# A pooled-and-banded attention kernel feeding a phase mixer: the pooled branch is added to the transposed banded one, the mixer works in 128-token chunks, and inputs are staged in pieces

## The chip, the cores and the metric

The kernel runs on one NeuronCore of a Trainium2 chip. TensorE (PE, with its weight loads shown apart as PEld) does the matrix products and writes to PSUM; VectorE (DVE) and ScalarE (ACT) read PSUM and SBUF; GpSimd (POOL) works in SBUF; SyncE (SP) issues the transfers. Each engine takes its instructions in the order in which they stand. The metric is the device time of one execution in microseconds.

## The reference

There are 8 batches of 8 heads, 576 tokens and 64 features per head. Two attentions are added, and the sum goes through a mixer over tokens and a product over channels:

```python
q_d, k_d, v_d = (t.reshape(B, H, 144, 4, 64).mean(axis=3) for t in (q, k, v))
out_up    = repeat(softmax(q_d @ k_d.T / 8) @ v_d, 4, axis=2)      # pooled by 4 tokens
out_local = softmax(where(|i - j| < 4, q @ k.T / 8, -1e9)) @ v     # banded
x = (out_up + out_local) as (B, 576, 512)
theta = x @ w_theta
zr, zi = x * cos(theta), x * sin(theta)
y = w_tok_r @ zr + w_tok_i @ zi                                    # over tokens
u = x + y
out = u + maximum(u @ w_ch, 0)
```

Inputs and output are float32; the kernel's products take bf16 and sum in float32.

## The kernel before, in words

Each batch passes through ten step functions, all of them generators whose every `yield` is one step. `load` issues the transfers of q, k and v, `cast` makes bf16 of them (GpSimd, in batch 0 also VectorE), `turns` transposes q and k by matmuls against a matrix `ip` that holds an identity and 24 pooling columns, so that each chunk of 96 tokens gives 96 transposed tokens and 24 pooled ones (lines 331 to 335). Batches 0 and 1 are read in another layout and are pooled by six more matmuls of 144 columns per pair of heads (line 312). `turns` ends with the pooled values, five matmuls of 512 columns (line 349).

`scores` makes the pooled scores in two groups of 90 and 54 keys (line 368), exponentiates them on ScalarE (lines 379, 388), then does the same for the band in five overlapping windows of 128 keys (lines 400, 408) and sets everything outside the band to zero by two selections on GpSimd (lines 421, 423), in batch 0 and part of batch 1 by one multiplication on VectorE. `pooled_out` multiplies the pooled weights with the pooled values (line 437, 32 matmuls per batch). `outputs` works in five chunks of 120, 120, 120, 120 and 96 tokens: one matmul of 512 columns spreads the pooled result over its tokens (line 462, `psup`), eight small ones give the banded result (line 467), and VectorE divides (476) and adds the two (483) to get `x`, tokens on partitions.

`transposes` turns `x` into `xT` (500, 505), `phases` multiplies by `w_theta` (517) and takes the cosine and the sine on ScalarE (524, 525), `modulate` multiplies both by `x` on VectorE (533). `mix` does the product over tokens: eight groups per batch, each of ten matmuls of 288 columns, five chunks times two matrices (553), and VectorE adds `xT` (559). `channels` multiplies by `w_ch` and transposes back (573, 578; the last 64 tokens as two halves side by side, 586 and 593), ScalarE clips at zero (598), and `store` adds and writes out (608, 610). `build_WT` loads, casts and transposes the two token matrices once (254 to 283).

What sets the order is written out by hand: strings of letters, `FIRST` and `SECOND` for the first two batches, `PERIOD` for each of the middle ones, `LAST` and `END`. Each letter takes one step of one function: `l`, `k`, `L` load, `C` cast, `A` turns, `S` scores, `N` pooled_out, `V` outputs, `T` transposes, `H` phases, `Z` modulate, `X` mix, `R` channels, `O` store, `W` the token matrices. `pin` ties every instruction to the one before it on its engine, so the letters fix the order on each engine. In a round for batch b the letters `X`, `R` and `O` stand for batch b-1, `A` for b+1, `C` for b+2 and `L` for b+3. PSUM has two tiles of two banks (`w2`) and four of one bank (`w1`), each handed out in turn.

## Time and profile before

| What | Value |
|---|---|
| Time, median of 3 runs | 298.91 us (298.89 to 298.97) |
| The profiled execution: its time, its span | 298.93 us, 297.2 us |
| Busy over the span: PE, DVE, ACT, POOL | 275.5, 204.1, 189.7, 159.5 us |
| Mean granted TensorE clock | 0.976 |
| DMA traffic | 43.57 MB, mean 147 GB/s |
| First mix matmul starts | 58.21 us |
| One middle batch, from its pooled values (line 349) to the next batch's | 31.34 us |

The busy time is that of an engine's instructions in one profiled execution. Matmuls overlap in the pipeline, so the mean length of one is longer than the time it takes up: the difference between the starts of consecutive groups gives that, and is called its slot below. The chain of waits follows the work that ended last back to the start; a table by stage gives each engine's busy time in a stretch of the span.

### The profile page before, as it was taken

How to read it: one execution, taken by the hardware profiler on the slowest of the kernel's cores; microseconds unless marked ns; L12 is line 12 of the kernel's file. 1: busy time of each engine (PE TensorE's matmuls, PEld its weight loads, DVE VectorE, ACT ScalarE, POOL GpSimd, SP SyncE). 2: the span in 40 equal slices, each digit the busy share in tenths (PEclk: the TensorE clock that was granted, in tenths of full speed). 3: DMA queues.
4: the chain of work that ended last, by engine and by line, in shares of the span. 5: the costliest groups of instructions: out<-in, count | busy, mean ns of one | idle time of the engine just before them, and what ended most of it. 6: DMA issues, size and time to landing. Idle time of an engine off the chain costs nothing.

```text
span 297.2 us, 7393 instructions
## 1 busy us (share of the span) xinstructions
PE 275.5 (93%) x2946; PEld 197.4 (66%) x2946; DVE 204.1 (69%) x466; ACT 189.7 (64%) x304; POOL 159.5 (54%) x186
## 2 busy tenths in 40 slices
PE   2497899999989999999999999999999999999993
PEld 1385587687656876587657876687668766776762
DVE  4433868657895598658883888468855986488642
ACT  1145458775668776776788667877787678565312
POOL 5666774478841399327960798059904900580000
PEclk9998579999999999999999999999999999999999
DMA  7999999999999953897189906992220012000304
GB/s 188 228 298 276 254 198 189 256 195 200 186 253 188 235 109 102 180 224 144 36 199 218 199 5 181 216 208 46 79 82 3 3 67 94 2 35 3 124 23 138
DMA packets 107826, 43.57 MB, mean 147 GB/s; under 512 B 97424, under 2 KB 101520, under 8 KB 107792
## 3 DMA queue, kind: packets, MB, share of 16 engines
q1 hardware_dynamic: 107792, 43.10, 69.4%
q8 instruction: 23, 0.38, 0.6%
q14 instruction: 11, 0.09, 0.1%
HBM read 33.65 MB, written 9.44 MB: 145 GB/s over the span
## 4 chain that ended last, share of the span: by engine, by line
PE 75%; DMA 7%; POOL 4%; SPq 4%; DVE 4%; ACT 2%; issue 1%; DVEq 0%; POOLq 0%; ACTq 0%
PE psu L553 26%; PE psth L517 11%; PE psr L573 8%; PE pstr L331 6%; PE psnd L437 4%; PE psS L400 3%; DMA q<-in_q_dram 3%; PE psvd L349 3%; SPq L107 3%; PE psloc L467 3%; PE psup L462 3%; PE xTps L500 2%; DMA w<-in_moe_w_theta_dram 2%; PE psx L578 2%; PE psSd L368 2%
## 5 line engine op out<-in xcount | busy, mean ns | idle before, releaser
L553 PE MATMUL psu<-WT,z 120*128 120x288 bf16 (+1 forms) x640 | 87.0, 286 | 0.2 <-ACT rel L598 0.2
L421 POOL TENSOR_SCALAR_AFFINE_SELECT pm<-pm 128x1024 bf16<-128x1024 bf16 (+1 forms) x32 | 33.7, 1053 | 73.7 <-ACT pm L408 73.6
L553 PEld LDWEIGHTS <-z 120*128 120x128 bf16 (+1 forms) x640 | 59.9, 98 | 15.9 <-issue 0.2
L408 ACT ACTIVATE pm<-psS 128x1024 bf16<-128x1024 f32 (+1 forms) x40 | 39.4, 984 | 18.0 <-PE psS L400 16.7
L559 DVE TENSOR_TENSOR uT<-psu,xT 128x288 bf16<-128x288 f32 x64 | 29.0, 454 | 26.2 <-PE psu L553 25.9
L517 PE MATMUL psth<-wth,xT 128*120 128x512 bf16 (+1 forms) x160 | 41.3, 381 | 0.2 <-DVE xT L505 0.2
L524 ACT ACTIVATE cs<-psth,pihc 120x512 bf16<-120x512 f32 (+1 forms) x40 | 27.4, 686 | 16.0 <-PE psth L517 13.8
L598 ACT ACTIVATE rel<-psr 128x512 f32<-128x512 f32 (+1 forms) x40 | 22.0, 554 | 23.1 <-PE psr L573 19.7
L423 POOL TENSOR_SCALAR_AFFINE_SELECT pm<-pm 128x1024 bf16<-128x1024 bf16 (+1 forms) x32 | 34.1, 1064 | 2.2
L573 PE MATMUL psr<-wch,uT 128*128 128x512 bf16 x128 | 33.0, 378 | 0.0
L608 DVE TENSOR_TENSOR osb<-rel,psx 128x512 f32<-128x512 f32 (+1 forms) x40 | 24.9, 630 | 7.6 <-ACT rel L598 7.6
L533 DVE TENSOR_TENSOR z<-cs,x 120x1024 bf16<-120x1024 bf16 (+1 forms) x40 | 29.2, 756 | 0.8 <-ACT cs L525 0.8
L476 DVE TENSOR_TENSOR tmp<-psloc,rl 120x512 bf16<-120x512 f32 (+1 forms) x40 | 27.6, 691 | 1.4
L483 DVE TENSOR_TENSOR x<-tmp,psup 120x512 bf16<-120x512 bf16 (+1 forms) x40 | 27.4, 686 | 1.4
L525 ACT ACTIVATE cs<-psth 120x512 bf16<-120x512 f32 (+1 forms) x40 | 23.5, 588 | 0.0
L517 PEld LDWEIGHTS <-xT 128*120 128x120 bf16 (+1 forms) x160 | 18.0, 131 | 7.9 <-DVE xT L505 0.7
L153 POOL CAST v_w<-v 128x1024 bf16<-128x1024 f32 x16 | 18.4, 1166 | 7.7 <-DMA v<-in_v_dram 5.2
L149 POOL CAST k_tm<-k 96x1024 bf16<-96x1024 f32 x18 | 18.3, 1040 | 7.7 <-DMA k<-in_k_dram 7.7
L334 ACT CAST kT<-pstr 128x384 bf16<-128x384 f32 x36 | 16.0, 483 | 9.8 <-PE pstr L331 9.8
L467 PEld LDWEIGHTS <-pm 128*128 128x128 bf16 (+1 forms) x320 | 16.6, 105 | 7.0 <-DVE tmp L476 1.9
L335 DVE CAST qdT<-pstr 128x96 bf16<-128x96 f32 x36 | 9.2, 256 | 16.1 <-ACT qT L334 14.8
L334 ACT CAST qT<-pstr 128x384 bf16<-128x384 f32 x36 | 16.2, 484 | 4.9 <-PE pstr L331 4.9
(89 smaller groups left out, 474.4 us busy)
## 6 DMA issues: line engine op xcount, KB each, us to landing
v<-in_v_dram SPq DMA_DIRECT2D x32, 256.0 KB, 5.8
out_dram<-osb SPq DMA_DIRECT2D x32, 256.0 KB, 2.2
q<-in_q_dram SPq DMA_DIRECT2D x36, 192.0 KB, 4.8
k<-in_k_dram SPq DMA_DIRECT2D x36, 192.0 KB, 5.1
q<-in_q_dram SPq DMA_DIRECT2D x8, 288.0 KB, 4.8
k<-in_k_dram SPq DMA_DIRECT2D x8, 288.0 KB, 6.9
v<-in_v_dram SPq DMA_DIRECT2D x8, 200.0 KB
...
```

What stands on the lines that cost most here:

```text
L334: nc.scalar.copy(out=To[:, :, TR * c:TR * c + TR], in_=ps[:, :, 0:TR])
L408: nc.scalar.activation(out=pv, in_=ps[0:kw].rearrange("p e (j w) -> p (e j) w", w=P)[:, :, 0:qn], func=AF.Exp, scale=SCL,)
L421: nc.gpsimd.affine_select(out=pv, in_=pv, compare_op=ALU.is_ge, fill=0.0, base=off, pattern=[[0, 8], [-1, qn]], channel_multiplier=1)
L423: nc.gpsimd.affine_select(out=pv, in_=pv, compare_op=ALU.is_ge, fill=0.0, base=6 - off, pattern=[[0, 8], [1, qn]], channel_multiplier=-1)
L476: nc.vector.tensor_tensor(out=tmp[0:cnt].rearrange("p (j e d) -> p e j d", e=2, j=4), in0=pv[0:cnt, :, :, 0:D], in1=rl[0:cnt].unsqueeze(3) ...
L483: nc.vector.tensor_tensor(out=x[0:cnt], in0=tmp[0:cnt], in1=up[0:cnt], op=ALU.add)
L517: nc.tensor.matmul(out=th[0:cnt, :], lhsT=xT[:, dc, QS[c]:QS[c] + cnt], rhs=wth[:, dc, :], start=(dc == 0), stop=(dc == 3),)
L524: nc.scalar.activation(out=cs[0:cnt, 0, :], in_=th[0:cnt], func=AF.Sin, bias=pihc[0:cnt], scale=1.0)
L533: nc.vector.tensor_tensor(out=z[0:cnt, c, :, :], in0=css.pop((b, c))[0:cnt], in1=xs[b][c][0:cnt].unsqueeze(1).to_broadcast([cnt, 2, DM]), ...
L553: nc.tensor.matmul(out=ps[:, 0:288], lhsT=z[0:QC[c], c, ri, P * dc:P * dc + P], rhs=WT[0:QC[c], ri, c, cols], start=(c == 0 and ri == 0), ...
L559: nc.vector.tensor_tensor(out=uT[:, dc, cols], in0=ps[:, 0:288], in1=xT[:, dc, cols], op=ALU.add)
L573: nc.tensor.matmul(out=psr, lhsT=uT[:, dc, P * c:P * c + P], rhs=wch[:, dc, :], start=(dc == 0), stop=(dc == 3),)
```

## The change

The functions keep their letters; what they do changes as follows.

- **Pooled keys.** The pooled keys are stored as four groups of 30 in slots of 32 and a fifth group of 24 (`kdP`). The fifth groups of all heads share one tile: for them 8 matmuls with 32 stationary columns each write one 32-partition strip. In batches 0 and 1 pooling is a sum on VectorE over the transposed tokens. For the others ScalarE, which already copies the transposed keys, also copies the pooled keys out of PSUM, in one or two pieces per chunk; VectorE did that before.
- **Pooled values.** Four matmuls of 512 columns and four of 128, each into its own 32-partition strip, in place of five of 512; GpSimd spreads the fifth group with two multiplications.
- **Pooled output.** `pooled_out` has 8 matmuls of 65 columns and 2 of 260 per group in place of 16 of 65, its stationary operand has 72 columns in place of 120. A third step transposes the result (8 matmuls of 72 columns) into `xdT`.
- **The sum of the two branches.** `psup` and the VectorE addition to `x` are gone. `transposes` turns the banded result alone, and the VectorE instruction that took it out of PSUM adds the pooled one, each column repeated over four tokens.
- **Chunks of 128.** `phases` and `modulate` work on 128 tokens, four chunks and one of 64. In the last, cosine and sine of the 64 tokens stand on the two halves of the partitions, one ScalarE instruction for both. Since `x` with tokens on partitions is no longer made, `modulate` transposes `xT` back (24 matmuls per batch) and VectorE multiplies out of PSUM. The mix has nine matmuls per group in place of ten.
- **Staging.** Inputs and weights come in pieces of up to 4 KB per partition through eight buffers used in turn, in place of one buffer each for q, k and v. In batch 0 VectorE casts q and ScalarE k, in batch 1 ScalarE q; ScalarE also casts `w_theta` and the second token matrix.
- **Order.** New strings, in which letters run on through all batches, with three periods. A new letter `D` issues six matmuls of 512 columns on zeros whose result nobody reads; it occurs ten times. `rel` and `osb` have two buffers in place of three.

The first place where the order differs in what the following speaks of is TensorE around the first mix matmul. Before, on TensorE (`psvd` holds the pooled values, `wps` the transposed token matrices, `pstr` the turns of q or k, `psSd` the pooled scores, `psu` the mix; the digit behind a name is the batch):

```order
L349 MATMUL psvd_1_877<-v_w_78,pu_154 54x512
L278 LDWEIGHTS wtm_199
L278 MATMUL wps_887<-ident,wtm_199 120x128
...
L278 MATMUL wps_896<-ident,wtm_199 96x64
...
L331 MATMUL pstr_2_920<-ip,q_tm_784 128x120
...
L368 MATMUL psSd_1_928<-qdT_494,kdT_90 90x144
...
L331 MATMUL pstr_2_936<-ip,q_tm_784 128x120
...
L553 MATMUL psu_0_944<-WT,z_577 128x288
```

And in the change, on TensorE (`psloc` is the banded output, `psth` the phases):

```order
L491 MATMUL psloc_1_1140<-v_w_95,pm_1_960 128x65
...
L541 MATMUL psth_1_1153<-wth,xT_944 128x512
...
L322 MATMUL pstr_2_1161<-ip,k_tm_668 128x120
...
L322 MATMUL pstr_2_1172<-ip,k_tm_668 128x120
...
L491 MATMUL psloc_1_1182<-v_w_95,pm_1_1085 96x65
...
L583 MATMUL psu_0_1196<-WT,z_744 128x288
```

So 568 matmuls stand ahead of the first mix in place of 439: all turns of batch 2 and the scores and outputs of batch 1 have moved ahead of it.

The second place is ScalarE in the turns of the keys of a middle batch. Before (`rel` is the clipped product, `cs` cosine and sine), ScalarE has one copy for each chunk of keys, and VectorE the pooled part (line 335):

```order
L334 CAST kT_1552<-pstr_3_1756 128x4x96
L334 CAST kT_1552<-pstr_3_1763 128x4x96
L408 ACTIVATE pm_2_1791<-psS_2_1782 128x1024
L334 CAST kT_1552<-pstr_3_1835 128x4x96
L408 ACTIVATE pm_2_1851<-psS_2_1842 100x8x96
L524 ACT_TABLE_LOAD
L524 ACTIVATE cs_2_1879<-psth_2_1874,pihc 120x512
```

In the change, on ScalarE, the keys of the same batch:

```order
L325 CAST kT_1327<-pstr_3_1561 128x4x96
L333 CAST kdP_91<-pstr_3_1561 128x4x24
L627 ACTIVATE rel_0_1598<-psr_0_1588 128x512
L325 CAST kT_1327<-pstr_3_1603 128x4x96
L333 CAST kdP_91<-pstr_3_1603 128x4x6
L333 CAST kdP_91<-pstr_3_1603 128x4x18
L325 CAST kT_1327<-pstr_3_1624 128x4x96
L333 CAST kdP_91<-pstr_3_1624 128x4x12 x2
L550 ACTIVATE cs_1_1652<-psth_1_1643,pihc 128x512
```

Behind each copy of keys stand one or two short copies of pooled keys out of the same PSUM tile, nine of them per batch, and VectorE's six are gone.

The third place is the end of TensorE's list (`psr` is the product with `w_ch`, `psx` the transposed `u`, `wu` the matmuls on zeros). Before:

```order
L573 MATMUL psr_7_5043<-wch,uT_4901 128x512
...
L578 MATMUL psx_7_5044<-ident,uT_4901 128x128
...
L586 MATMUL psr_7_5055<-wch,uT_4901 64x256
...
L593 MATMUL psx_7_5056<-ident,uT_4901 64x128
L701 UNCONDITIONAL_BRANCH
```

And in the change:

```order
L602 MATMUL psr_7_5135<-wch,uT_4951 128x512
...
L607 MATMUL psx_7_5136<-ident,uT_4951 128x128
L275 LDWEIGHTS ident
L275 MATMUL wu_5150<-warm,ident 128x512
...
L615 MATMUL psr_7_5157<-wch,uT_4951 64x256
...
L622 MATMUL psx_7_5158<-ident,uT_4951 64x128
...
L275 MATMUL wu_5173<-warm,ident 128x512
```

Six matmuls on zeros stand ahead of the last product of the kernel and six behind it; of the other eight groups of six, five stand ahead of the first mix and three behind it.

The diff, cut to what is spoken of here:

```diff
+    stg = ctx.enter_context(tc.tile_pool(name="stg", bufs=8))
...
+    def stage(b, key):
+        t = staged[b, key] = stg.tile([P, 1024], FP32, tag="st", name=f"st{b}_{key}")
+        return t
...
+    dve, act, gp = nc.vector.tensor_copy, nc.scalar.copy, nc.gpsimd.tensor_copy
+    CASTS = {0: (dve, act, gp), 1: (act, gp, gp), None: (gp, gp, gp)}
...
+    def warm_up():
+
+        for i in range(WARM):
+            ps = w1(f"wu{i}")
+            for _ in range(6):
+                nc.tensor.matmul(out=ps, lhsT=ident, rhs=warm, start=True, stop=True)
+            yield
+
+    warm = const.tile([P, 512], BF16, name="warm")
+    nc.vector.memset(warm, 0.0)
+    WARM = 10
 
...
+                if n == 0:
+                    nc.vector.tensor_reduce(out=qdT[:, hh, :], in_=To[:, hh, :].rearrange("p (m j) -> p m j", j=4),
+                                            axis=AX.X, op=ALU.add)
+                else:
+                    nc.vector.tensor_reduce(out=kdP[:, hh, 0:4, 0:30],
+                                            in_=To[:, hh, 0:480].rearrange("p (g m j) -> p g m j", g=4, j=4),
+                                            axis=AX.X, op=ALU.add)
+                    nc.vector.tensor_reduce(out=kdP[:, hh, 4, 0:24], in_=To[:, hh, 480:576].rearrange("p (m j) -> p m j", j=4),
+                                            axis=AX.X, op=ALU.add)
...
-            nc.vector.tensor_copy(out=Tdo[:, :, TP * c:TP * c + TP], in_=ps[:, :, TR:TW])
+            if n == 0:
+                dve(out=qdT[:, :, TP * c:TP * c + TP], in_=ps[:, :, TR:TW])
+            elif c == 5:
+                nc.scalar.copy(out=kdP[:, :, 4, 0:TP], in_=ps[:, :, TR:TW])
+            else:
+                for g in range(TP * c // 30, (TP * c + TP - 1) // 30 + 1):
+                    lo, hi = max(TP * c, 30 * g), min(TP * c + TP, 30 * g + 30)
+                    nc.scalar.copy(out=kdP[:, :, g, lo - 30 * g:hi - 30 * g],
+                                   in_=ps[:, :, TR + lo - TP * c:TR + hi - TP * c])
...
+        psa, psb = w1(f"psva_{b}"), w1(f"psvb_{b}")
+        for c in range(4):
+            nc.tensor.matmul(out=psa[KP * c:KP * c + KP, :], lhsT=PU[min(c, 1)], rhs=v_w[:, c, :, 0:D],
+                             start=True, stop=True)
+        for c in range(4):
+            nc.tensor.matmul(out=psb[KP * c:KP * c + KP, 0:2 * D], lhsT=PU[1][0:KW[4], :],
+                             rhs=v_w[0:KW[4], 4, c::4, 0:D], start=True, stop=True)
+        nc.scalar.copy(out=vd[:, 0, :, 0:D], in_=psa.rearrange("p (h d) -> p h d", d=D))
+        last4 = work.tile([P, 2, D], BF16, tag="last4", bufs=1, name=f"last4_{b}")
+        nc.scalar.copy(out=last4, in_=psb[:, 0:2 * D].rearrange("p (s d) -> p s d", d=D))
+        for s in range(2):
+            nc.gpsimd.tensor_tensor(
+                out=vd[:, 1, 4 * s:4 * s + 4, 0:D],
+                in0=last4[:, s, :].unsqueeze(1).to_broadcast([P, 4, D]),
+                in1=own.unsqueeze(2).to_broadcast([P, 4, D]),
+                op=ALU.mult,
...
+        pooled_scores(lambda par: ps[:, par, 0:SD], 3)
+        for h in range(H):
+            par, r = h % 2, KP * (h % 4)
+            nc.tensor.matmul(
+                out=ps[r:r + KP, h // 4, SD:2 * SD],
+                lhsT=kdP[64 * par:64 * par + 64, h // 2, 4, :],
+                rhs=qdT[64 * par:64 * par + 64, h // 2, :],
+                start=True, stop=True,
             )
...
-                for kk in range(2):
-                    nc.tensor.matmul(
-                        out=pv[0:120, h // 4, h % 4, :],
-                        lhsT=pd[:, kk, h, 24 * g:24 * g + 120],
-                        rhs=vd[:, kk, h, 0:65],
-                        start=(h % 4 == 0 and kk == 0), stop=(h % 4 == 3 and kk == 1),
-                    )
...
+                nc.tensor.matmul(
+                    out=pv[:, h // 4, h % 4, :],
+                    lhsT=pd[:, h, QD * g:QD * g + QD], rhs=vd[:, 0, h, 0:65],
+                    start=(h % 4 == 0), stop=False,
+                )
+            for e in range(2):
+                nc.tensor.matmul(
+                    out=pv[:, e, :, :],
+                    lhsT=pd[:, H + e, QD * g:QD * g + QD], rhs=vd[:, 1, 4 * e:4 * e + 4, 0:65],
+                    start=False, stop=True,
+                )
...
+        ps = w1(f"psxd_{b}", BF16)[:, 0:4 * SD].rearrange("p (e w) -> p e w", w=SD)
+        for dc in range(4):
+            for g in range(2):
+                nc.tensor.transpose(out=ps[:, dc, QD * g:QD * g + QD], in_=xd[:, g, P * dc:P * dc + P],
+                                    identity=ident[0:QD, 0:QD])
+        xds[b] = work.tile([P, 4, SD], BF16, tag="xdT", name=f"xdT{b}")
+        nc.vector.tensor_copy(out=xds[b], in_=ps)
...
-            up = w1(f"psup{c}_{b}")
-            o = QS[c] - 96 * (c == 4)
-            nc.tensor.matmul(out=up[0:qn, :], lhsT=rt[:, o:o + qn], rhs=xd[:, c // 4, :], start=True, stop=True)
...
-            nc.vector.tensor_tensor(out=x[0:cnt], in0=tmp[0:cnt], in1=up[0:cnt], op=ALU.add)
...
-            nc.vector.tensor_copy(out=xT[:, :, QS[c]:QS[c] + cnt], in_=ps[:, :, 0:cnt])
...
+            nc.vector.tensor_tensor(
+                out=xT[:, :, QS[c]:QS[c] + cnt].rearrange("p e (m j) -> p e m j", j=4),
+                in0=ps[:, :, 0:cnt].rearrange("p e (m j) -> p e m j", j=4),
+                in1=xdT[:, :, QS[c] // 4:(QS[c] + cnt) // 4].unsqueeze(3).to_broadcast([P, 4, cnt // 4, 4]),
+                op=ALU.add,
+            )
...
+            n = OC[c]
...
+                for lo in range(0, P, n):
+                    nc.tensor.matmul(
+                        out=th[lo:lo + n, :], lhsT=xT[:, dc, P * c:P * c + n], rhs=wth[:, dc, :],
+                        start=(dc == 0), stop=(dc == 3),
+                    )
...
+            if c < 4:
+                nc.scalar.activation(out=cs[:, 0, :], in_=th, func=AF.Sin, bias=pihc[:, 0:1], scale=1.0)
+                nc.scalar.activation(out=cs[:, 1, :], in_=th, func=AF.Sin, bias=0.0, scale=1.0)
+            else:
+                nc.scalar.activation(out=cs[:, 0, :], in_=th, func=AF.Sin, bias=pihc[:, 1:2], scale=1.0)
...
+            for dc in range(4):
+                for lo in range(0, P, n):
+                    nc.tensor.transpose(out=ps[lo:lo + n, P * dc:P * dc + P], in_=xT[:, dc, P * c:P * c + n], identity=ident)
+            m = 2 if c < 4 else 1
             nc.vector.tensor_tensor(
-                out=z[0:cnt, c, :, :], in0=css.pop((b, c))[0:cnt],
-                in1=xs[b][c][0:cnt].unsqueeze(1).to_broadcast([cnt, 2, DM]),
+                out=z[:, 2 * c:2 * c + m, :], in0=ps.unsqueeze(1).to_broadcast([P, m, DM]),
+                in1=css.pop((b, c))[:, 0:m, :],
...
-                for c in range(NCH):
-                    for ri in range(2):
-                        nc.tensor.matmul(
-                            out=ps[:, 0:288],
-                            lhsT=z[0:QC[c], c, ri, P * dc:P * dc + P],
-                            rhs=WT[0:QC[c], ri, c, cols],
-                            start=(c == 0 and ri == 0), stop=(c == NCH - 1 and ri == 1),
-                        )
+                for j in range(9):
+                    nc.tensor.matmul(
+                        out=ps[:, 0:288], lhsT=z[:, j, P * dc:P * dc + P], rhs=WT[:, j, cols],
+                        start=(j == 0), stop=(j == 8),
+                    )
...
     PERIOD = (
-        "SSXXAXSAASAANXANASAAXVSAAXSTCVXASCCVHXCCTVROHTCVRLOHTRZHOTCCLLRLZOZZHCRZSOLLLLLL"
+        "SCXZZZSXROLACCASLXAROASXRALOVANLRAVOLAXLSVCCAATXSTVACRTLSOTVCHXXHCLTHZNLACHZHNA"
     )
```

441 lines of the change are left out of this document (183 added, 258 removed).

## The prediction

> **What bounds the kernel now.** I read the page first, then the chain of waits, then a table by stage, then TensorE's list in order of time.
>
> ```profile
> PE 275.5 (93%) x2946; PEld 197.4 (66%) x2946; DVE 204.1 (69%) x466; ACT 189.7 (64%) x304; POOL 159.5 (54%) x186
> PE 75%; DMA 7%; POOL 4%; SPq 4%; DVE 4%; ACT 2%; issue 1%; DVEq 0%; POOLq 0%; ACTq 0%
> ```
>
> TensorE is busy for 93% of the span and makes three quarters of the chain. That is an average, so the stages come next. The columns are the stretch, its length, busy time of each engine with its instructions, the granted clock, the DMA share and GB/s.
>
> ```profile
> 0.00:58.21 58.21, 43.97 (x441) 33.60 (x442) 34.58 (x84) 26.86 (x42) 36.98 (x67) 0.88 1.10 237
> 58.21:292.60 234.39, 231.47 (x2507) 163.84 (x2505) 168.69 (x382) 162.51 (x263) 122.51 (x119) 1.00 0.61 124
> 154.33:185.67 31.34, 31.34 (x351) 22.39 (x352) 23.32 (x55) 23.71 (x40) 19.82 (x19) 1.00 0.77 155
> 30.00:40.00 10.00, 8.59 (x85) 6.52 (x85) 7.69 (x15) 4.65 (x6) 7.24 (x10) 0.50 1.10 236
> ```
>
> The kernel has two parts. Until the first mix matmul at 58.21 us the DMA engines are full (237 GB/s), and TensorE is busy for 43.97 us of it, for a stretch at half its clock. From there to 292.60 us TensorE is busy for 231.47 of 234.39 us, and in a middle batch without a gap: 31.34 of 31.34 us, while VectorE and ScalarE have 8.0 and 7.6 us free. So the second part is worth what TensorE's instructions take up, the first what loading and preparing take. Behind 292.60 us lie 4.6 us for the last output, and the execution's own 298.93 us lies 1.73 us above its span of 297.2 us and 0.02 us above the median.
>
> **The price of TensorE's groups.** The length of a matmul in the records is no price, since they overlap. The start of the next group minus the start of this one is. TensorE's list in a middle batch, with the start, the modelled length and the group:
>
> ```profile
> 154.26 1.39 PE L349 MATMUL psvd<-v_w,pu 128*90 128x512 bf16 x5
> 155.58 0.57 PE L368 MATMUL psSd<-qdT,kdT 64*90 64x144 bf16 x12
> 156.09 2.63 PE L553 MATMUL psu<-WT,z 120*128 120x288 bf16 x20
> 158.55 0.37 PE L331 MATMUL pstr<-ip,q_tm 96*128 96x120 bf16 x4
> 158.76 1.39 PE L553 MATMUL psu<-WT,z 120*128 120x288 bf16 x10
> ...
> 161.63 1.02 PE L437 MATMUL psnd<-vd,pd 90*120 90x65 bf16 x16
> 162.48 1.39 PE L553 MATMUL psu<-WT,z 120*128 120x288 bf16 x10
> ...
> 167.08 0.38 PE L462 MATMUL psup<-xd,rt 120*128 120x512 bf16 x1
> 167.30 0.40 PE L467 MATMUL psloc<-v_w,pm 128*128 128x65 bf16 x8
> 167.63 0.40 PE L400 MATMUL psS<-qT,kT 64*128 64x128 bf16 x8
> 167.96 0.59 PE L331 MATMUL pstr<-ip,k_tm 96*128 96x120 bf16 x8
> ...
> 178.25 0.51 PE L467 MATMUL psloc<-v_w,pm 100*96 100x65 bf16 x8
> 178.60 1.03 PE L573 MATMUL psr<-wch,uT 128*128 128x512 bf16 x4
> 179.46 0.39 PE L578 MATMUL psx<-ident,uT 128*128 128x128 bf16 x4
> 179.69 1.03 PE L517 MATMUL psth<-wth,xT 128*120 128x512 bf16 x4
> ...
> 183.97 1.03 PE L517 MATMUL psth<-wth,xT 128*96 128x512 bf16 x4
> 184.93 0.63 PE L586 MATMUL psr<-wch,uT 128*64 128x256 bf16 x8
> 185.39 0.28 PE L593 MATMUL psx<-ident,uT 128*64 128x128 bf16 x4
> 185.60 0.63 PE L349 MATMUL psvd<-v_w,pu 128*90 128x512 bf16 x2
> ```
>
> From these: a mix matmul 0.123 us (20 in 2.46); one of 512 columns 0.215 (4 in 0.86); the spreading one 0.22; pooled output 0.053 (16 in 0.85); pooled values 1.32 for five; pooled scores 0.043; scores and banded output 0.041 (8 in 0.33); the banded output with 96 stationary columns 0.044; a turn 0.053 (4 in 0.21); a transpose of 128 columns 0.056 (4 in 0.23). The eight halves of 256 columns take 0.46 us; one after the other, at the mix's rate of 0.123 us for 288 columns, they would take 0.87. So two outputs on different halves of the partitions run side by side, a pair in 0.115 us. The four half transposes take 0.21 us, so they don't.
>
> **The second part, term by term**, by the instructions that stand behind the first mix matmul, from 231.5 us:
>
> - Mix: 640 matmuls become 576; 64 x 0.123 = 7.9 off.
> - The 35 spreading matmuls go; 35 x 0.22 = 7.7 off.
> - Pooled output: 14 groups at 0.85 become 12 (two more run ahead of the mix), each 8 x 0.044 + 2 x 0.111 (260 columns at the mix's rate) = 0.57; 11.9 to 6.8, 5.1 off. The nearest row for 72 stationary columns is the one with 96; in proportion to columns it would be 0.49 a group, another 1.0.
> - Pooled values: six batches at 1.32 = 7.9. Now four strips of 512 columns and four of 128: one after the other 4 x 0.215 + 4 x 0.055 = 1.08, all four at once 0.28. The row of the halves shows that two run at once, 0.58; I take 0.45, so 2.7, 5.2 off (between 1.4 and 6.2).
> - Pooled scores: 106 matmuls become 96, 0.4 off; if the eight narrow ones of a batch get no partner they cost 0.062 each in place of 0.043, 0.9 in all.
> - Phases: 140 x 0.215 = 30.1 become 108 x 0.215 + 28 pairs x 0.23 = 29.6, 0.5 off (in sequence the 56 halves would take 12.0 in place of 6.4).
> - Work moved ahead of the first mix: 40 turns (2.1), 40 scores (1.6), 40 banded outputs (1.6), 8 transposes (0.4), together 5.7 off.
> - Added: 48 transposes of 72 columns, by the row of 65 columns 0.041 each, 1.9; 168 transposes back to tokens at 0.056 and, for the halves, 0.053: 9.2.
>
> That is 32.5 off and 11.1 on: **231.5 becomes 210.1 us**. A middle batch falls from 31.3 to about 29.3 us.
>
> Four groups of matmuls on zeros stand in this part ahead of the last product, 24 x 0.215 = 5.2 us, and before the change TensorE waited 2.9 us here (234.39 - 231.47). Zeros that stand where TensorE would wait cost nothing. I take 6.5 us for both: below, 2.9; above, 8.1, and more if the waits grow. The fifth group stands behind the last output and is covered by its transfer.
>
> Of the other engines, VectorE loses the addition to `x` and the pooled keys and has to put out `xT` with an addition. Even if that and the multiplication out of PSUM run at one element a cycle it stays below its 23.3 us per batch, so I cost it at nothing: its cover is TensorE's 29.3 us. ScalarE loses one sine, one exponential and half of a copy, and gains nine short copies of pooled keys.
>
> ```profile
> L408 ACT ACTIVATE pm<-psS 128x1024 bf16<-128x1024 f32 x32 | 32.9, 1027 | 15.5 <-PE psS L400 14.2 <-POOL pm L421 1.2
> L334 ACT CAST qT<-pstr 128x384 bf16<-128x384 f32 x36 | 16.2, 484 | 4.9 <-PE pstr L331 4.9
> L379 ACT ACTIVATE pd<-psSd 90x864 bf16<-90x864 f32 x16 | 13.5, 884 | 0.1
> L408 ACT ACTIVATE pm<-psS 100x768 bf16<-100x768 f32 x8 | 6.5, 812 | 2.5 <-PE psS L400 2.5
> L324 ACT CAST qT<-pstr 128x576 bf16<-128x576 f32 x8 | 5.1, 639 | 9.3 <-PE pstr L312 9.0
> L322 ACT CAST kdT<-pstr 128x144 bf16<-128x144 f32 x4 | 1.1, 279 | 9.8 <-DVE kT L321 9.8
> L525 ACT ACTIVATE cs<-psth 120x512 bf16<-120x512 f32 x32 | 18.9, 589 | 0.0
> L524 ACT ACTIVATE cs<-psth,pihc 120x512 bf16<-120x512 f32 x32 | 22.0, 687 | 12.3 <-PE psth L517 10.2 <-issue 1.8 <-ACT cs L525 0.2
> L524 ACT ACT_TABLE_LOAD x8 | 10.3, 1283 | 3.0 <-PE psth L517 2.9
> ```
>
> A copy of 144 elements took 0.279 us and one of 384 0.484, so 24 to 96 elements cost about 0.2: nine are 1.8, against 0.59 + 0.88 + 0.3 taken away. ScalarE keeps its 23.7 us, now in 29.3: 81% in place of 76%.
>
> **The first part.** Before the first mix SP's list must have brought, up to the third piece of keys of batch 2, batches 0 and 1 whole, six pieces of batch 2, `w_theta`, both token matrices and half of `w_ch`.
>
> ```profile
> q<-in_q_dram SPq DMA_DIRECT2D x36, 192.0 KB, 4.8
> ```
>
> Six such transfers are a batch's q, 1.18 MB, so a batch has 3.54 MB. The sum is 2 x 3.54 + 6 x 0.39 + 1.05 + 2.65 + 0.52 = 13.7 MB, at 237 GB/s 57.6 us, and the cast and the turn behind it add 1.5: 59. ScalarE's work ahead of it, at the prices above: eight casts of 768 at 0.81, seven for weights 5.3, twelve copies at 0.64 and ten at 0.48, 1.4 for pooled keys, 1.7 for values, 3.1 and 9.8 for the exponentials, 5.8 for cosine and sine, three tables at 1.28: 50 us, where before it had 26.86. Begun at about 4.6 us it ends at 55 if it never waits. So two queues of nearly the same length meet, each waiting for the other now and then; I take **61 us** for the first mix, between 57 and 68. TensorE's 36 us of slots ahead of it fit.
>
> Together: 61 + 210.1 + 6.5 + 4.6 + 1.7 = **284 us**.
>
> **Rivals.**
>
> *The strips don't run side by side, or each change to them empties the array.* Against it stands the pair in 0.115 us. For it: behind the products of 183.97, whose slot ends at 184.83, the halves begin only at 184.93, 0.10 us lost. The change has four new stretches of strips or halves per batch, so eight changes, 0.8 us; over seven batches 5.6. All strips in sequence would give 3.8 (values) + 5.6 (phases) + 0.9 (scores) = 10.3. So 290 to 300, most likely 294. The Trainium skill, page TensorEngine Tiling (Array Packing), section Key Properties, says that changing the tiling mode drains TensorE; the trace agrees with a loss, of 0.10 us here.
>
> *A late start.* Eight staging buffers are given back by casts that stand in line behind other work, ScalarE's among them; with a cast late, SP's next load is late, and everything behind it in the list. The clock speaks for it too: at 30 to 40 us it was 0.50, and TensorE's 36 us of slots at that clock would be 72. Five groups of zeros stand against that. A first mix at 68 to 76 us gives 291 to 299. The Trainium skill's page TensorE: Matmul & The Clock Gate, Part 1, has the clock at half after an idle window of about 3.4 us; the 0.50 agrees.
>
> *Slower than before: ScalarE's hand-offs set the pace.* The tile of a key turn is now read by two or three copies on ScalarE in a row, 0.7 to 0.9 us, where two engines shared it. If the six turns and the phases each make TensorE wait, 3 us a batch are lost: 284 + 7 x 3 = 305. It decides against the change from 2.1 us a batch on (14.9 / 7). Against it: ScalarE has 5.6 us free per batch.
>
> *More than forecast*: loads at the DMA's floor with the first mix at 57, strips four wide, zeros inside waits: 57 + 208 + 3 + 6.3 = 274.
>
> **How the numbers follow.** The forecast, 276 to 291, has 0.66; the better case below 276 0.12; strips in sequence 0.06; the late start 0.10; slower by ScalarE 0.06. The range of 273 to 295 leaves out half of the better case's lower end and the cases above 295. Less than 0.2%, 0.6 us, can't be told from no change. Faster: 0.66 + 0.12 + 0.06 + 0.08 = 0.92; slower 0.06 + 0.01; same 0.01.
>
> **What would show it.** The first mix matmul at 57 to 68 us; middle batches at 29 to 30 us with TensorE without gaps; 576 mix matmuls at 0.123; the four strips of values in 0.3 to 0.6 us; ScalarE near 24 us per batch. The prediction is wrong if TensorE shows waits for ScalarE of more than 1 us per batch, if the halves of the phases take 1.7 us per batch, or if the first mix comes after 70 us.

## The result, and the profile after

The changed kernel takes 286.78 us (median of 4 runs, 284.61 to 287.70); the kernel before, on the same chip, 298.90 us (298.17 to 298.97). The ratio is 0.9589 [0.9532, 0.9647]: about 12 us faster, against a forecast of 284.0 us and a range of 273 to 295. Run again later, beside a kernel before of 302.05 us, it took 288.65 us, ratio 0.9494 [0.941, 0.9578]. Medians are of all executions of a kernel and ratios of its fast ones alone; of these later four, two, the profiled one among them, were over 1.5% longer than the fastest, and so was one of the four of the kernel with the even turns first.

The profiled execution of 287.7 us has a span of 286.0 us. First the page (busy time of the engines; then the chain of work that ended last, its shares by engine):

```profile
PE 262.6 (92%) x3022; PEld 179.9 (63%) x3022; DVE 186.2 (65%) x422; ACT 196.2 (69%) x355; POOL 145.4 (51%) x170
PE 79%; DMA 8%; DVE 6%; ACT 3%; POOL 1%; issue 1%; SPq 0%; POOLq 0%
```

TensorE has 12.9 us less work in the records (275.5 before). The split used in the forecast, at the first mix matmul, has moved from 58.21 to 68.92 us. The table of stretches, with the same columns as before (stretch, length, busy time and instructions of PE, PEld, DVE, ACT and POOL, granted clock, DMA share, GB/s):

```profile
0.00:68.92 68.92, 48.80 (x568) 31.52 (x569) 48.51 (x128) 47.85 (x76) 32.86 (x52) 0.95 1.10 228
68.92:281.64 212.72, 212.36 (x2453) 147.94 (x2452) 137.26 (x293) 148.05 (x280) 112.54 (x118) 1.00 0.56 129
121.41:150.88 29.47, 29.47 (x367) 20.78 (x365) 19.83 (x45) 23.40 (x48) 20.15 (x22) 1.00 0.72 165
55.00:60.00 5.00, 3.32 (x46) 2.47 (x43) 2.89 (x9) 4.07 (x10) 2.37 (x3) 0.88 1.25 232
60.00:65.00 5.00, 5.00 (x45) 3.44 (x44) 2.87 (x7) 2.17 (x8) 3.77 (x4) 0.50 0.94 197
```

So the first part became 10.7 us longer, the second, up to the last product, fell from 234.39 to 212.72 us, and a middle batch from 31.34 to 29.47 us. TensorE's waits behind the first mix matmul are gone: the view of waits holds one line for that stretch.

```profile
PE psth L541 <- DVE osb L636: 0.3, 1, 0.3
```

TensorE's list in a middle batch (start, modelled length, group) gives the new prices by the same reading, start to start:

```profile
125.36 0.41 PE L491 MATMUL psloc<-v_w,pm 128*128 128x65 bf16 x8
125.70 0.40 PE L346 MATMUL psva<-v_w,pu 128*32 128x512 bf16 x4
125.92 0.23 PE L349 MATMUL psvb<-v_w,pu 100*32 100x128 bf16 x4
126.09 1.04 PE L602 MATMUL psr<-wch,uT 128*128 128x512 bf16 x4
...
127.66 0.31 PE L396 MATMUL psSd<-qdT,kdP 64*32 64x144 bf16 x8
127.90 0.38 PE L521 MATMUL xTps<-ident,tmp 120*128 120x120 bf16 x4
...
133.66 0.44 PE L453 MATMUL psnd<-vd,pd 128*72 128x65 bf16 x8
133.94 0.39 PE L459 MATMUL psnd<-vd,pd 128*72 128x260 bf16 x2
134.17 0.38 PE L322 MATMUL pstr<-ip,q_tm 96*128 96x120 bf16 x4
...
135.24 0.39 PE L562 MATMUL psxt<-ident,xT 128*128 128x128 bf16 x4
135.56 1.05 PE L541 MATMUL psth<-wth,xT 128*64 128x512 bf16 x8
136.54 0.47 PE L453 MATMUL psnd<-vd,pd 128*72 128x65 bf16 x8
...
137.71 1.28 PE L583 MATMUL psu<-WT,z 128*128 128x288 bf16 x9
138.83 0.95 PE L562 MATMUL psxt<-ident,xT 128*128 128x128 bf16 x16
139.71 0.40 PE L414 MATMUL psS<-qT,kT 64*128 64x128 bf16 x8
```

The four strips of pooled values with 512 columns take 0.22 us together, the price of one alone (0.215 in the prediction's list); the four short ones 0.17. Eight narrow pooled scores take 0.24 us, 0.030 each. A group of pooled output takes 0.28 + 0.23 = 0.51. The four pairs of half phases take 0.98, or 0.245 a pair. Nine mix matmuls take 1.12 us, and sixteen transposes back 0.88; eight of the sixteen are whole and eight have 64 columns.

What took the first part to 68.92 us is in the chain that ended last (start, length, what), the stretch from the last two pieces of the token matrices on:

```profile
49.15 6.61 DMA stw_tok<-in_moe_w_tok_i_dram
...
55.78 0.67 ACT wtm L248
...
56.83 0.58 ACT wtm L248
...
57.45 0.66 PE wps L262 x6
...
69.09 0.98 PE psu L583 x8
```

The transfer lands at 55.8 us, two casts and a copy on ScalarE follow, and from 57.45 us TensorE works without a gap for 11.5 us on turns of the token matrices, turns, scores and phases that stand ahead of the mix in its list. The row of 60 to 65 us shows it at half its clock in that stretch.

### The profile page after: what moved, and what is told of

It is laid out like the page before. It is cut to its first block, busy times and chain, and to the rows that moved or that the text cites. A ratio compares the mean times of both kernels' runs of the same rounds, so it can differ in the third digit from the quotient of the medians.

```text
span 286.0 us, 7570 instructions
## 1 busy us (share of the span) xinstructions
PE 262.6 (92%) x3022; PEld 179.9 (63%) x3022; DVE 186.2 (65%) x422; ACT 196.2 (69%) x355; POOL 145.4 (51%) x170
## 4 chain that ended last, share of the span: by engine, by line
PE 79%; DMA 8%; DVE 6%; ACT 3%; POOL 1%; issue 1%; SPq 0%; POOLq 0%
PE psu L583 25%; PE psth L541 12%; PE psr L602 10%; PE pstr L322 5%; PE psS L414 3%; PE psloc L491 3%; PE psxt L562 3%; DMA st_q<-in_q_dram 3%; PE xTps L521 3%; DMA st_k<-in_k_dram 3%; PE psx L607 2%; DMA stw_tok<-in_moe_w_tok_i_dram 2%; PE wu L275 2%; PE psr L615 2%; PE wps L262 2%; DVE kdP L312 1%
## 5 line engine op out<-in xcount | busy, mean ns | idle before, releaser
L583 PE MATMUL psu<-WT,z 128*128 128x288 bf16 x576 | 79.5, 286 | 0.0
L583 PEld LDWEIGHTS <-z 128*128 128x128 bf16 x576 | 53.4, 98 | 15.3
L541 PE MATMUL psth<-wth,xT 128*128 128x512 bf16 (+1 forms) x192 | 42.0, 389 | 0.3 <-DVE osb L636 0.3
L547 ACT ACTIVATE cs<-psth,pihc 128x512 bf16<-128x512 f32 x32 | 22.0, 688 | 17.2 <-PE psth L541 15.5
L139 POOL CAST v_w<-st_v 128x1024 bf16<-128x1024 f32 (+1 forms) x24 | 21.3, 896 | 17.7 <-DMA st_v<-in_v_dram 14.1
L522 DVE TENSOR_TENSOR xT<-xTps,xdT 128x480 bf16<-128x480 bf16 (+1 forms) x40 | 25.3, 632 | 7.5 <-PE xTps L521 7.4
L564 DVE TENSOR_TENSOR z<-psxt,cs 128x1024 bf16<-128x1024 bf16 (+1 forms) x40 | 24.6, 632 | 8.5 <-PE psxt L562 5.2
L133 POOL CAST k_tm<-st_k 96x1024 bf16<-96x1024 f32 x18 | 18.4, 1036 | 10.8 <-DMA st_k<-in_k_dram 8.1
L133 POOL CAST q_tm<-st_q 96x1024 bf16<-96x1024 f32 x18 | 18.4, 1034 | 3.9 <-DMA st_q<-in_q_dram 3.9
L548 ACT ACTIVATE cs<-psth 128x512 bf16<-128x512 f32 x32 | 18.9, 592 | 0.0
```

Source lines behind the costliest of these rows:

```text
L133: eng[i](out=dst[:, 2 * c:2 * c + 2].rearrange("p c h d -> p (c h d)"), in_=staged.pop((b, f"{'qk'[i]}{c}"))[0:TR])
L522: nc.vector.tensor_tensor(out=xT[:, :, QS[c]:QS[c] + cnt].rearrange("p e (m j) -> p e m j", j=4), in0=ps[:, :, 0:cnt].rearrange("p e (m j) ...
L541: nc.tensor.matmul(out=th[lo:lo + n, :], lhsT=xT[:, dc, P * c:P * c + n], rhs=wth[:, dc, :], start=(dc == 0), stop=(dc == 3),)
L583: nc.tensor.matmul(out=ps[:, 0:288], lhsT=z[:, j, P * dc:P * dc + P], rhs=WT[:, j, cols], start=(j == 0), stop=(j == 8),)
```

## The experiments

All ratios are to the kernel before, run beside each kernel. "First mix" is the start of the first mix matmul; "second part" in this section is the span from there to its end (217.1 us in the changed kernel, with the last output).

**Term one: 64 mix matmuls.** A tenth matmul, on zeros, is put into each of the 64 mix groups.

```diff
-                        start=(j == 0), stop=(j == 8),
+                        start=(j == 0), stop=False,
                     )
+                nc.tensor.matmul(out=ps[:, 0:288], lhsT=z[:, 8, P * dc:P * dc + P], rhs=warm[:, 0:288],
+                                 start=False, stop=True)
```

> The changed kernel with a tenth matmul of 288 columns, on zeros, in each of the 64 groups of the mix. If TensorE's slots set the second part, it grows from 217.1 by 64 x 0.12 = 7.7-7.9 us, to about 225, and the ratio rises by 0.026. If TensorE has slack there, or ScalarE sets the pace, it grows by less than 4 us.

293.38 us (293.08 to 293.73), ratio 0.9724 [0.969, 0.9757]. First mix at 67.11, span 292.0, so a second part of 224.9 us: 7.8 us more, 0.122 for each. In TensorE's list the tenth lies between the groups and takes 0.12 us:

```profile
130.82 0.29 PE L587 MATMUL psu<-warm,z 128*128 128x288 bf16 x1
130.94 1.27 PE L583 MATMUL psu<-WT,z 128*128 128x288 bf16 x9
```

The largest term taken off, 7.9 us for 64 mix matmuls, holds.

**Term two: the spreading matmuls**, taken out of the kernel before alone.

```diff
-            up = w1(f"psup{c}_{b}")
-            o = QS[c] - 96 * (c == 4)
-            nc.tensor.matmul(out=up[0:qn, :], lhsT=rt[:, o:o + qn], rhs=xd[:, c // 4, :], start=True, stop=True)
...
-            nc.vector.tensor_tensor(out=x[0:cnt], in0=tmp[0:cnt], in1=up[0:cnt], op=ALU.add)
-            xs[b].append(x)
+            xs[b].append(tmp)
```

> The kernel before without the spreading matmul of the pooled output and without the addition of it to x on VectorE: the pooled branch is left out of the result. It is one term of the prediction alone: 35 x 0.22 = 7.7 us off the second part (234.4 us to the last product), 8.6 us in all with the five of the first part if these lay on the path. Rival: TensorE's free slots are filled by waits for something else (VectorE's x, GpSimd), and 4 us or less come off; or the ones in the first part lie under loads, and it is 7.7 alone.

291.39 us (289.27 to 293.56) beside 300.6 us, ratio 0.966 [0.9603, 0.9718]. The same group of two successive batches, first in this kernel, then in the kernel before:

```profile
143.46 1.02 PE L568 MATMUL psr<-wch,uT 128*128 128x512 bf16 x4
173.68 1.02 PE L568 MATMUL psr<-wch,uT 128*128 128x512 bf16 x4
```

```profile
144.54 1.02 PE L573 MATMUL psr<-wch,uT 128*128 128x512 bf16 x4
175.88 1.02 PE L573 MATMUL psr<-wch,uT 128*128 128x512 bf16 x4
```

A batch falls from 31.34 to 30.22 us: 1.12 for five, 0.224 each, as priced. Over the whole second part (first mix at 58.80, span 291.2) 6.6 us come off and not 7.8; a new wait stands behind the first mix:

```profile
PE psloc L464 <- DVE pm L414: 2.0, 1, 2.0
```

In this profile the first part did not get shorter (58.80 against 58.21). But it is of the longest of the four executions (293.56 us), and the median one is 9.2 us below the kernel before beside it, so whether the five matmuls there lay under loads is not settled.

**Term three: the transposes back**, each issued twice.

```diff
-                for lo in range(0, P, n):
+                for lo in list(range(0, P, n)) * 2:
```

> The changed kernel with each transpose back to tokens issued twice into the same place; the result is the same. 168 of these stand behind the first mix matmul. The prediction's term: 168 x 0.055 = 9.2 us, so a second part of 217.1 + 9.2 = 226.3 us and a middle batch of 29.47 + 24 x 0.055 = 30.8 us. Rival: part of the transposes lies where TensorE would stand anyway, in the last batches, or a longer turn makes VectorE late with z: 5 us or less, or 11 and more with new waits.

294.17 us (292.1 to 295.02), ratio 0.9766 [0.9709, 0.9823]. First mix at 68.57, span 293.3: second part 224.7 us, 7.6 more. In a middle batch:

```profile
121.11:151.69 30.58, 30.58 (x394) 21.89 (x391) 19.89 (x45) 23.56 (x48) 19.91 (x22) 1.00 0.76 158
```

and in TensorE's list:

```profile
140.90 1.62 PE L562 MATMUL psxt<-ident,xT 128*128 128x128 bf16 x32
142.45 0.40 PE L414 MATMUL psS<-qT,kT 64*128 64x128 bf16 x8
```

24 more transposes take 1.11 us, 0.046 each; the group of 16 went from 0.88 to 1.55 (140.90 to 142.45). TensorE is busy for all of the batch and no wait came with them, so the transposes are on the path. Their mean price hides two. A group of halves alone, ahead of the first mix, shows it, first in the changed kernel, then with each half issued twice:

```profile
66.69 0.41 PE L562 MATMUL psxt<-ident,xT 128*64 128x128 bf16 x8
67.04 0.42 PE L491 MATMUL psloc<-v_w,pm 128*128 128x65 bf16 x8
```

```profile
66.11 0.64 PE L562 MATMUL psxt<-ident,xT 128*64 128x128 bf16 x16
66.68 0.42 PE L491 MATMUL psloc<-v_w,pm 128*128 128x65 bf16 x8
```

Eight more halves take 0.57 - 0.35 = 0.22 us, 0.055 a pair, as much as one whole transpose. So two halves run side by side. The prediction had read the opposite from four halves in 0.21 us; two pairs would be 0.11 of that, and the rest is of the size of the loss at a change of the tiling (see the rival by the strips below). 112 whole transposes and 28 pairs at 0.055 make 7.7 us: that is the 7.6 measured, where the prediction's term was 9.2.

**Term four: the groups of zeros.** In one kernel the five groups of the second part go, by leaving out the letter D in the last string (its first line shown), in another those of the first part too, by leaving it out everywhere.

```diff
-    WARM = 10
+    WARM = 5
...
-        "AXSZDRZSOZCSXAALRSXOXCNACRVAOVDSATAVXVAXARORAOSXXTASRTOSSROXSTVHXHVXTXNRZHOVHZNRRHOOSZZDSNZTROROTVXX"
+        "AXSZRZSOZCSXAALRSXOXCNACRVAOVSATAVXVAXARORAOSXXTASRTOSSROXSTVHXHVXTXNRZHOVHZNRRHOOSZZSNZTROROTVXXHVT"
```

> The changed kernel without the five groups of matmuls on zeros behind the first mix. If they take slots from TensorE where it has no wait, four of them cost 4 x 1.29 = 5.2 us: the time falls by 4 to 5.5 us, to 281.5-283. If they stand in places where TensorE would wait anyway, the time stays within 1.5 us of 286.8, and TensorE shows about 4 us of waits in place of the zeros. If they hold the clock, it falls below 1.00 somewhere behind 200 us and the time rises.

282.99 us (280.77 to 284.63), ratio 0.9408 [0.9326, 0.9491]. First mix at 66.08, span 280.4, so a second part of 214.3 us: 2.8 less, where the 24 slots ahead of the last product make 5.2. Up to the last product TensorE's list became 3.9 us shorter (212.65 to 208.74); a new wait of 0.6 us, for VectorE's `tmp`, is in it. Behind the last product the span grew from 4.4 to 5.6 us, since VectorE now waits for a transfer out of `osb` (2.00 us in the chain) before it can write the last piece. TensorE's last group, first in this kernel, then in the changed one:

```profile
274.61 0.28 PE L622 MATMUL psx<-ident,uT 128*64 128x128 bf16 x4
```

```profile
281.36 0.28 PE L622 MATMUL psx<-ident,uT 128*64 128x128 bf16 x4
```

So a part of the zeros stood where something else would have been waited for.

> The changed kernel without all ten groups of matmuls on zeros. If the five early ones hold the clock in the first part, the clock falls to half earlier and for longer than the 9 us around 60 us, and the first mix comes later than 69 us: against the run without the late ones alone the time rises by 2 to 6 us. If they don't, their 6.4 us stand in slack and the first mix stays at 68 to 69 us.

285.76 us (283.93 to 286.66), ratio 0.9489 [0.943, 0.9548]; first mix at 69.73, second part 214.4. The second part is the same as with the early zeros. The first is 3.7 us longer, with a clock of 0.60 at 55 to 60 us and 0.50 at 60 to 65, which is what zeros that hold the clock would do. But the changed kernel, which has the early zeros, shows nearly the same clock and a start of 68.92, and the intervals of the two ratios overlap. No gain or loss of the early zeros can be told.

**The late start: which work stands between the last load and the mix?** Three kernels change the order. In the first the turns of the first token matrix stand ahead of those of the second, so that less waits for the second's casts.

```diff
-        for j in range(9):
+        for j in (0, 2, 4, 6, 1, 3, 5, 7, 8):
```

> The changed kernel, but the turns of the first token matrix stand ahead of those of the second (order 0, 2, 4, 6, 1, 3, 5, 7, 8). Theory A (the first mix is late because TensorE stands at the first turn of the second matrix from 55.5 to 57.45 us, waiting for a ScalarE cast, and then runs at half clock until about 66.5): the wait and the half clock go, the first mix moves from 68.9 to 63-65 us, and the time falls by 3 to 6 us from 286.8, to 281-284. Rival B (loading alone sets the first mix; the clock costs nothing because TensorE has slack there): the first mix stays at 67 us or later, and the time within 1.5 us of 286.8.

286.51 us (285.74 to 290.68), ratio 0.9513 [0.9452, 0.9575], whose interval overlaps the changed kernel's. The first mix came at 66.97 us:

```profile
58.30 0.52 PE L262 MATMUL wps<-ident,wtm 128*128 128x128 bf16 x5 [1.10 <-DVE qdT L327]
...
66.97 1.27 PE L583 MATMUL psu<-WT,z 128*128 128x288 bf16 x9
```

```profile
60.00:65.00 5.00, 5.00 (x76) 3.49 (x75) 4.48 (x12) 4.19 (x13) 3.76 (x5) 1.00 0.94 189
```

The second fence is the table of stretches: TensorE still waits ahead of a group of turns, now 1.10 us for VectorE, but the clock stayed whole, and TensorE's row from that wait to the mix took 8.7 us. In the changed kernel nearly the same row took 11.5. So about 2.8 of its 68.92 us belong to the clock, and the order of the turns is worth nothing that can be told.

In the second the token matrices are loaded (l) ahead of batch 2's pieces (L), and one cast of them (c) goes ahead of one of batch 2's (C).

```diff
-        "LCLLCLACALCLCAALACLCLLALLlCALASCCSSCASSDVCNlLcLVCCNcLACCLlDLLLLcCAAAANLClllCSLADAClClASTClScLcSVTSlS"
-        "LCTAVHVLCTcHZHTZlcClNLcZlcAHVAZANLcLWACSDcNALDcLCTSCWWAAVAWWAWLCWACTWSLLHVWZVHAcClALVXLTSXCLSTXACZSS"
+        "LCLLCLACALCLCAALACLCLLALLlCALASCCSSCASSDVCNlLcLVCCNcLACCLlDLLLLcCAAAANLClllCSlADAClClASTClSclcSVTSlS"
+        "LCTAVHVLcTCHZHTZLcCLNLcZlcAHVAZANLcLWACSDcNALDcLCTSCWWAAVAWWAWLCWACTWSLLHVWZVHAcClALVXLTSXCLSTXACZSS"
```

> The changed kernel, but the loads of the token matrices stand ahead of the first four loads of batch 2. By theory A the second token matrix is cast about 3 to 6 us earlier (1.6 MB at 237 GB/s stood ahead of it), TensorE waits less at its first turn, and the first mix moves to 63-66 us, the time to 282-285. By the rival that batch 2's turns, which also stand ahead of the first mix, are the later ones, TensorE now waits at them instead and the time stays within 1.5 us of 286.8.

290.09 us (288.09 to 291.39), ratio 0.9635 [0.9571, 0.9698]; the first mix at 72.64, later than in any other kernel. The theory fell, and TensorE's list and the table of stretches show why:

```profile
53.45 0.38 PE L459 MATMUL psnd<-vd,pd 128*72 128x260 bf16 x1 [6.00 <-POOL vd L355]
```

```profile
50.00:55.00 5.00, 1.35 (x10) 1.04 (x10) 0.53 (x2) 0.00 (x0) 3.21 (x5) 0.61 0.89 199
```

GpSimd reached its cast of batch 2's q, whose load was now late, and stood there for 5.0 us. The spreading of the pooled values (`vd`, line 355) is behind it in GpSimd's list; TensorE waited 6.0 us for it and ScalarE 6.1 us for TensorE. Part of the delay is again the clock (0.61 in the row shown, 0.71 in the next five microseconds). In the third, batch 2's casts (C) and turns (A) are moved behind too, with the even turns first and the late zeros gone; of the first string the second line shows it:

```diff
-        "LCTAVHVLCTcHZHTZlcClNLcZlcAHVAZANLcLWACSDcNALDcLCTSCWWAAVAWWAWLCWACTWSLLHVWZVHAcClALVXLTSXCLSTXACZSS"
+        "TAVHVLTcHLZHTZcLNcLZcCLHVZNcCLLSNDcSCTLDWCLWVAWTcCAWAHVZWACAWCAWLAAWASlALWAVHCcVLAClXLTSXCLSTXACZSS"
```

> The changed kernel without the late zeros, with the token matrices loaded ahead of batch 2, and with the casts and turns of batch 2 moved behind batch 1's pooled values and the token matrices' turns, so that GpSimd and TensorE do not stand at batch 2's data. If the standing at batch 2's casts was what made the first mix later when the token matrices alone were moved (72.6 us), it now comes at 62 to 66 us, and the time at 278-282 us on a chip where the kernel before takes 298.9. If the first part is set by all the bytes that must land ahead of the first mix, whatever their order, it stays at 66 to 69 us.

285.95 us (284.54 to 287.24), ratio 0.948 [0.9436, 0.9523]; span 283.9. The wait for GpSimd is gone, and yet the first mix comes at 68.89. Two rows of its chain, and two of TensorE's list:

```profile
59.69 1.28 ACT L550
...
65.55 1.28 ACT L422
```

```profile
68.30 0.55 PE L491 MATMUL psloc<-v_w,pm 100*96 100x65 bf16 x8 [1.04 <-DVE pm L428]
68.89 1.27 PE L583 MATMUL psu<-WT,z 128*128 128x288 bf16 x9
```

The chain holds no load behind 40 us; it runs through ScalarE, VectorE and TensorE in turn, with three of ScalarE's table loads of 1.28 us and two groups of zeros (2.5 us) in it. With the loads out of the way, the hand-offs take as long.

**Both sides of that, apart.** The second token matrix isn't loaded at all; the casts read the first one's.

```diff
+                if ri == 0:
-                nc.sync.dma_start(out=stage("w", f"tok{ri}{ct}")[0:OC[ct], 0:S], in_=w[P * ct:P * ct + OC[ct], :])
+                    nc.sync.dma_start(out=stage("w", f"tok{ri}{ct}")[0:OC[ct], 0:S], in_=w[P * ct:P * ct + OC[ct], :])
...
-                (gp, act)[ri](out=w_tm[ri][0:OC[ct], ct, :], in_=staged.pop(("w", f"tok{ri}{ct}"))[0:OC[ct], 0:S])
+                src = staged.pop(("w", f"tok{ri}{ct}"))[0:OC[ct], 0:S] if ri == 0 else w_tm[0][0:OC[ct], ct, :]
+                (gp, act)[ri](out=w_tm[ri][0:OC[ct], ct, :], in_=src)
```

> The changed kernel without the five loads of the second token matrix (1.33 MB, about 5.7 us at the 232 GB/s of this stretch); its casts read the first matrix's bf16 copy instead, so the result is of two equal token matrices. Every engine's other instructions stay. In the changed kernel the fourth piece of this matrix landed at 55.8 us and TensorE's row of turns, scores and phases behind it (8.7 us at full clock, 11.5 where the clock was halved) ended at the first mix matmul, 66 to 71 us over the runs so far. Theory A (the start is the last load plus the work behind it): the first mix comes at 61 to 64 us, the second part stays at 217.1 us, about 5 us less in all. Rival B (the hand-offs between ScalarE, VectorE and GpSimd in this part take as long as the loads, as the run with the token loads moved ahead hints, where the chain of waits held no load behind 40 us and the mix still began at 68.9): the first mix comes at 66 us or later and the time moves by 1 us at most.

283.31 us (282.5 to 286.58), ratio 0.9436 [0.937, 0.9502]; span 281.2. The first mix came at 64.21 us, just outside theory A's 61 to 64 and ahead of rival B's 66, and the second part is 217.0. From 50.62 us on TensorE has next to no wait left: it is busy for 13.50 of the 13.59 us up to the first mix (two rows of the table of stretches, then the first mix in TensorE's list):

```profile
50.00:55.00 5.00, 4.86 (x54) 2.91 (x53) 3.37 (x10) 4.97 (x9) 1.88 (x3) 1.00 1.23 223
55.00:60.00 5.00, 4.91 (x75) 3.90 (x75) 4.52 (x13) 4.15 (x14) 4.07 (x4) 1.00 1.09 191
```

```profile
64.21 1.27 PE L585 MATMUL psu<-WT,z 128*128 128x288 bf16 x9
```

Against the starts of the unchanged order with the clock whole behind 50 us (66.08 and 67.11 in the table below) 5.7 us of transfer gave 1.9 to 2.9 us; against the changed kernel's own 68.92 it is 4.7, of which the clock has 2.8. So both sides hold in part. The last load did make TensorE wait, 0.96 and 0.71 us in the changed kernel; once it is gone, TensorE's own row sets the start. Two groups of zeros, 1.3 us each, stand in this row; what they cost here was not tested.

**The rival by ScalarE: the copies of pooled keys on VectorE.**

```diff
-                nc.scalar.copy(out=kdP[:, :, 4, 0:TP], in_=ps[:, :, TR:TW])
+                dve(out=kdP[:, :, 4, 0:TP], in_=ps[:, :, TR:TW])
```

(and the same for the other eight of a batch)

> The changed kernel with the short copies of the pooled keys on VectorE in place of ScalarE (9 of about 0.25 us a batch); the result is the same. The prediction had one rival in which these copies, a row of ScalarE hand-offs behind each key turn, cost 2 to 3 us a batch. If that held, a middle batch falls from 29.47 to about 27 us and the time by 10 us or more. By the forecast's own reason (TensorE full, ScalarE at 23.4 of 29.5 us) the middle batch stays at 29.4 to 29.5 us and the time within 1.5 us.

290.03 us (289.21 to 292.17), ratio 0.965 [0.9593, 0.9706]. The rival falls, but so does the forecast's "within 1.5 us": the first mix comes at 66.05, the span is 287.5, and the second part 221.5 us, 4.4 longer. A middle batch in the table of stretches, and the wait in TensorE's list:

```profile
118.36:148.82 30.46, 29.85 (x365) 20.91 (x365) 20.71 (x54) 22.56 (x37) 20.53 (x23) 1.00 0.76 163
```

```profile
148.82 1.04 PE L602 MATMUL psr<-wch,uT 128*128 128x512 bf16 x4 [0.47 <-DVE osb L636]
```

VectorE has 0.9 us more work a batch, and 9.7 us free, and yet the batch is 1.0 us longer: `osb`, behind the copies in VectorE's list, gives its PSUM buffer back later and TensorE's next product waits. With the gap around it this stop is 0.6 of the 1.0 us; the rest lies in two short gaps behind it, whose cause was not read. That the copies were put on ScalarE matters by 1 us a batch.

**Repeats and the best version.** The changed kernel itself, and the one with both edits shown above, even turns first and no late zeros:

> The changed kernel itself, unaltered, beside the others of this call: a ratio of 0.955 to 0.962 to the kernel before, a first mix matmul at 66 to 70 us and 217 us from there to the end of the span. If the first mix differs by 2 us or more between profiles of the same instructions, differences of that size in the first part are no effect of an edit.

288.65 us, as told above; in the profiled execution, the longest of the four (289.6 us), the first mix is at 70.85 and the second part 217.05.

> The changed kernel with both edits: the first matrix's turns first, and no matmuls on zeros behind the first mix. If the two are independent: 2.8 us less behind the first mix (214.3 us), as without the late zeros alone, and a first mix at about 66-67 us with the clock at full; a ratio of 0.940 to 0.946 to the kernel before. If the order of the turns does nothing, the same as without the late zeros alone, 0.941 within its interval.

283.74 us (282.07 to 284.56), ratio 0.9401 [0.9359, 0.9442], beside the changed kernel's 0.9494 [0.941, 0.9578]; first mix at 68.53, second part 214.3. The gain of the late zeros repeats: 2.8 us in the second part. This version and the one without late zeros alone (0.9408) can't be told apart and are the fastest that ran.

The starts of the kernels whose list on TensorE up to the first mix is the same as in the changed one (but for the transposes issued twice), with the granted clock from the tables of stretches:

| kernel | first mix, us | clock at 40-45, 55-60, 60-65, 65-70 us |
|---|---|---|
| copies of pooled keys on VectorE | 66.05 | 1.00, 1.00, 1.00, 1.00 |
| no late zeros | 66.08 | 0.50, 1.00, 1.00, 1.00 |
| tenth mix matmul | 67.11 | 1.00, 1.00, 1.00, 1.00 |
| transposes twice (24 more ahead of the mix) | 68.57 | 1.00, 0.80, 0.52, 1.00 |
| changed | 68.92 | 1.00, 0.88, 0.50, 0.93 |
| changed again | 70.85 | 1.00, 1.00, 0.58, 0.74 |

Where the clock was whole from 55 us on, the starts lie at 66.05 to 67.11; where it was about half at 60 to 65 us, at 68.57 to 70.85.

## Why the prediction was right, and where not

The time lay in the range, 2.8 us above the forecast. The sum's parts against the profiled execution of 287.7 us:

| term | predicted | measured |
|---|---|---|
| first mix matmul | 61 | 68.92 |
| second part's slots, zeros and waits, to the last product | 210.1 + 6.5 | 207.2 + 5.5 |
| behind it, to the span's end | 4.6 | 4.4 |
| around the span | 1.7 | 1.7 |

So 7.9 us too few were added in one place and 3.9 too many in another. That the two partly cancel is luck: each alone is larger than the 2.8 us by which the forecast missed.

**The first mix matmul is the step that was mis-sized.** That "the cast and the turn behind it add 1.5" was wrong. The loads were not what was off: the floor gave 57.6 us for all of them, and the last pieces of the token matrices, which stand near the end of that list, were there at 55.8. But TensorE's list has, between the turn of those pieces and the first mix matmul, a row of turns, scores, banded output and phases that can only be worked off behind it, since an engine takes its instructions in order. With the clock whole nearly the same row measured 8.7 us, in the kernel with the even turns first; the other 2.8 are the half clock. From the landing to the first mix lay 13.1 us, about 10.3 of them without the half clock, against 1.5 and a lump of 2 us for queues that wait for each other. The order of instructions showed that row; it was counted as slots ("TensorE's 36 us of slots ahead of it fit") and not by its place. The start of 68.92 lies outside the 57 to 68 that the prediction gave for it, and ahead of the 70 us that it named as a sign of being wrong.

The rival of the late start named the time of the start (68 to 76) but not its cause. It had two: a cast that comes late and so a late load, and the clock. Against its floor the load was not late; what it made TensorE wait is worth 1.9 to 2.9 us by the kernel without it, and the clock 2 to 3 us. The time it gave, 291 to 299, did not come, because the second part was lower.

**The second part's slots came out 2.5 to 2.9 us below the sum.** 32.5 off and 11.1 on were 210.1 us of slots. TensorE was busy for 212.36 us there; less four groups of zeros at 1.29 that is 207.2, and in the kernel without the late zeros it was busy for 207.63. A middle batch, which has no zeros, was about 29.3 by the sum and 29.47 in the trace, so the difference is to be sought in the first and last batches; it was not traced further. Of the single terms, the mix (7.9; 7.8 measured with a tenth one) and the spreading (0.22 each; 0.224) were tested by themselves and hold. The transposes back were put at 9.2 and are 7.6 when doubled, because their halves run in pairs. By the list alone, pooled values are 0.39 us a batch for 0.45, pooled output 0.51 for 0.57, the pairs of phases 0.245 for 0.23; these were read, not tested apart.

**Zeros and waits** were taken at 6.5; in the trace the zeros take 5.2 and the waits 0.3. The waits that the kernel before had in this part (2.9 us) did not come back. In time the two cost less, 2.8 when the zeros left and the 0.3, which is near the prediction's lower bound of 2.9: zeros that stand where something would wait anyway cost nothing, as it said.

**The rival by the strips** falls in its larger part: the four strips of values run in the time of one. But the loss at a change of the tiling is there, and at the strips too. Eight banded outputs take 0.34 us ahead of the strips (125.36 to 125.70) and 0.24 where whole products follow:

```profile
118.78 0.41 PE L491 MATMUL psloc<-v_w,pm 128*128 128x65 bf16 x8
119.02 0.37 PE L322 MATMUL pstr<-ip,k_tm 96*128 96x120 bf16 x4
```

The four transposes ahead of the half phases take 0.32 (135.24 to 135.56), where four take 0.22 otherwise. So about 0.10 us was lost at each, as the rival had it. Prices read from start to start contain such losses, the prediction's too: its 0.33 us for eight banded outputs (167.30 to 167.63) stands ahead of scores with 64 rows. So the sum already held some of them, and a middle batch came out near it.

**The rival by ScalarE** falls: no wait of TensorE for ScalarE is left behind the first mix, with ScalarE at 23.40 of 29.47 us. The reason given was the free share, and the same reason fails for VectorE: with 9.7 us free it made a batch 1.0 us longer when it took the copies. What counts is what stands behind the added work in that engine's list. "I cost it at nothing" on VectorE came out right (19.83 us a batch, down from 23.3), but its free time was not what made it right.

**What stays open:** why the clock was halved in some executions at 55 to 65 us and not in others. The kernel with the copies on VectorE was busy for only 3.02 of the 5 us from 55 us on and kept 1.00; the changed kernel, with 3.32, did not. The spread of the first mix at full clock, 66 to 67 us, is not explained further, nor where the second part's slots fell below the sum.
